# SSM backward by quarters of D, interleaved by priority with the FFN weight-gradient pass; output gradient kept in SBUF; positions split 64x32

## The chip, the cores and the metric

The kernel runs on one core of a Trainium2 chip. The metric is the device time of one execution in microseconds (us). Three executions of the kernel before took 2714.63, 2717.66 and 2719.81 us; the median is 2717.66 us.

## What is computed

The reference is one layer and its gradients, for one sequence of L = 2048 positions, D = 576 channels, N = 128 states per channel and F = 4608 hidden units, all in bfloat16:

```python
xn = layernorm(x)                                   # no weights
K[d,l] = Re( sum_n C[d,n] * exp(dt*A[d,n]*l) * dt*B[d,n] )
s = causal_conv(xn, K) + xn * Dskip                 # by FFT of length 2L in the reference
g = silu( (silu(xn @ w1) * (xn @ w3)) @ w2 )
out = x + s * g
# then the vector-Jacobian product of out with grad_out, with respect to
# x, A_re, A_im, B_re, B_im, C_re, C_im, log_dt, Dskip, w1, w3, w2
```

The outputs are `out` (out_0), the gradient of x (out_1), the gradients of the eight SSM parameters (out_2 to out_9) and those of the three weight matrices (out_10 to out_12).

## The kernel before

The kernel is written in a framework that takes tiles from pools with a fixed number of buffers, finds the dependencies between instructions, orders the instructions of each engine by a priority and sets the semaphores. The order on each engine's queue is fixed before the kernel runs, and every queue is worked off in order. A call of `at(us)` (L81) sets the priority of the instructions that follow it, as a planned time; where no such call is made, program order counts. A tile that is allocated waits for the release of what lay at its address.

Positions are split for the SSM kernel K as l = 128*a + b, with AV = 16 values of a and BV = 128 values of b (L36, L54). For each chunk of 16 channels (36 chunks) a tile of QW + PW = 16*128 + 16*16 = 2304 columns of exponentials (`E_k`, L384 to L387, written to memory early) and of sines and cosines (`kgen_chunk`, L428: the matmul L439, the mask `m_k` on VectorE L440, three passes of ScalarE in `trig`, L294 to L298) is multiplied to `q_k` (the b part, stored to `Q_dram`) and `p_k` (the a part, stored through `pz_k`, which GpSimd makes at L453 and L454, to `PZ_dram`). The matmuls `kps` (L467) give K.

The program runs in these stages, whose times below are read from the trace.

- 0 to 110 us: parameters, layer norm. 110 to 243: `ssm_early` (L359), the exponentials and the spectra `UH_dram` of the input.
- 243 to 920: `ssm_forward` (K by chunks, then the convolution in blocks of 512 by DFT matmuls, L525 and L541, with the complex products of `cmul_acc`, L553, on VectorE) and `ffn_hidden` (L639) are interleaved by `at`.
- 948 to 1105: `ffn_output` (L687), 16 tiles of 128 positions. It forms the output gradient `go_o` and its transpose `gT` (L746, L749), writes them to `GO_dram` and `GOT_dram` (L736, L750), and writes `gs_t` for the SSM side to `GS_dram` (L739).
- 1115 to 1395: `phase5_conv_bwd` (L767), in two halves of 288 channels: DFT of `gs` (L525), products `Z` (L558 to L566) on VectorE, inverse DFT (L541) into `gKK` (the gradient of K) and, with the spectra of K, into the gradient of xn (`gx`, L849 to L851, stored to `GXN_dram`).
- 1395 to 1629: `param_sums` (L862): for each of the 36 chunks `qT` is loaded from `Q_dram` by a transposing DMA (L977), 32 matmuls `pT` of 32 columns sum over b (L879), and VectorE multiplies by `pz` and sums over a (L884, L886) into `S_all`. Then `phase5_final` (L889) makes the parameter gradients.
- 1629 to 2318: `phase6_weights` (L979), the FFN weight-gradient pass, in 18 groups of 256 hidden units: `go_oT` and `go_o` are loaded; per group `phase6_elementwise` (L1005) loads `gg_n` and `h_n`, applies SiLU and its derivative, computes `ph` from `go_oT` and `w2T` (L1038) with five matmuls for each of 16 tiles of positions (four of 128 rows, a tail of 64), and stores `gu_n`, `gg_n` to `GU_dram`, `GG_dram` (L1044); `phase6_weight_grads` (L1047) of the group before follows with the accumulations L1061, L1072, L1079 and L1081. `e_in` has three buffers, so the loads of a group need not wait for the group before; `e_ps_gw` has four PSUM banks.
- 2318 to the end: `phase6_inputs` (L1088): `w1T` and `w3T` are loaded by 72 transposing DMAs of 128 columns of a weight matrix each (L977 from the loop over `fi`), then 16 tiles of 144 matmuls (L1116) and the layer-norm backward.

All transposing DMAs are issued by the SP queue, in order with SP's other loads and stores.

## Time and profile before

| | |
|---|---|
| median of three executions | 2717.66 us |
| the profiled execution: its own time | 2719.59 us |
| its span, first to last instruction | 2717.6 us |
| mean granted TensorE clock | 0.828 |
| TensorE (PE) busy | 2024.5 us, 74% |
| VectorE (DVE) busy | 1418.1 us, 52% |
| ScalarE (ACT) busy | 929.7 us, 34% |
| GpSimd (POOL) busy | 519.0 us, 19% |

All numbers of the trace come from one execution. A row of the windows view gives a stretch of the span, its length, the busy time of each engine in it with the number of its instructions, the granted TensorE clock, the mean busy share of the DMA engines and their rate. A row of the groups gives a line, an engine, an operation and its tiles, the count, the busy time of the group and the mean time of one in ns, and the idle time ahead of it with what ended it. A row of the timeline gives a start, a duration and an instruction.

### The profile page before, as it was taken

Reading aid. Unit: us, or ns where it says so; the run is one execution under the profiler, and the core shown is the slowest. Engines: PE = TensorE matmul, PEld = TensorE weight load, DVE = VectorE, ACT = ScalarE, POOL = GpSimd, SP = SyncE. Lnnn points to the kernel's source line nnn. Section 1 sums busy time; section 2 is a strip of 40 time slices with the busy share of each in tenths; the row PEclk is TensorE's granted clock in tenths of the full one; section 3 lists DMA queues with packets and bytes.
Section 4 is the critical chain, followed back from the end, with each engine's and each line's share of the span. In section 5 each row is a group of like instructions: output and inputs, shape, how many; then the busy total and the mean of one; then the engine's idle time right before and its main releaser. Section 6 shows DMA issues by size and latency. Waiting matters only on the chain.

```text
span 2717.6 us, 37783 instructions
## 1 busy us (share of the span) xinstructions
PE 2024.5 (74%) x14886; PEld 1289.5 (47%) x14886; DVE 1418.1 (52%) x2396; ACT 929.7 (34%) x1203; POOL 519.0 (19%) x763
## 2 busy tenths in 40 slices
PE   1797777878799699636343325999999999129998
PEld 0332322322255277424233312777777778127777
DVE  7312666766687445597978892433333332002222
ACT  1356677777755211212100003444444441000000
POOL 1001454554533411000000000222222222000000
PEclk9555888887899899868665556999999999569999
DMA  3245656666665798323179947655555552488873
GB/s 74 81 191 220 230 203 238 236 220 236 222 232 185 216 236 212 88 63 95 55 176 237 233 106 208 177 158 152 166 166 168 151 153 64 102 164 176 169 165 73
DMA packets 678742, 455.04 MB, mean 167 GB/s; under 512 B 491426, under 2 KB 631972, under 8 KB 669220
## 3 DMA queue, kind: packets, MB, share of 16 engines
q1 hardware_dynamic: 541780, 246.58, 36.6%
q0 software_dynamic: 31824, 109.16, 11.8%
q10 hardware_dynamic: 104960, 96.90, 11.2%
q8 instruction: 116, 1.90, 0.3%
q14 instruction: 62, 0.51, 0.1%
HBM read 132.12 MB, written 209.24 MB: 126 GB/s over the span
## 4 chain that ended last, share of the span: by engine, by line
PE 37%; DVE 9%; DMA 8%; SPq 4%; issue 1%; ACT 0%; POOL 0%; ACTq 0%; DVEq 0%; POOLq 0%
PE px L1116 10%; PE pgw L1072 9%; PE ph L1038 8%; DMA qT<-Q_dram 6%; PE pgw L1061 5%; SPq L977 4%; DVE cm_t L564 1%; PE et_ps L525 1%; PE pgw L1079 1%; DVE Z L562 1%; PE inv_ps L541 1%; DVE cm_t L561 1%; DVE Z L565 1%; DVE Z L566 1%; PE pT L879 1%
## 5 line engine op out<-in xcount | busy, mean ns | idle before, releaser
L1116 PE MATMUL px<-w1T,ggc 128*128 128x288 bf16 x1152 | 236.5, 287 | 103.3 <-DMA ggc<-GG_dram 103.3
L1038 PE MATMUL ph<-w2T,go_oT 128*128 128x256 bf16 (+1 forms) x1440 | 228.9, 282 | 54.8 <-issue 40.4
L1116 PE MATMUL px<-w3T,guc 128*128 128x288 bf16 x1152 | 236.3, 287 | 4.6 <-DMA guc<-GU_dram 4.6
L1072 PEld LDWEIGHTS <-xn_bf 128*128 128x128 bf16 x2304 | 225.4, 98 | 27.0 <-issue 0.8
L671 PE MATMUL pg<-wmB_w,xnT 128*128 128x512 bf16 x576 | 178.7, 432 | 68.8 <-ACT g_t L678 44.5
L671 PEld LDWEIGHTS <-xnT 128*128 128x128 bf16 x1152 | 112.0, 105 | 234.0 <-issue 161.4
L1038 PEld LDWEIGHTS <-go_oT 128*128 128x128 bf16 (+1 forms) x1440 | 117.6, 98 | 164.3 <-issue 117.9
L1120 DVE TENSOR_TENSOR gx<-px,gx 128x288 f32<-128x288 f32 x32 | 13.2, 453 | 329.7 <-PE px L1116 329.7
L671 PE MATMUL pu<-wmB_w,xnT 128*128 128x512 bf16 x576 | 180.7, 430 | 2.0 <-ACT u_t L679 2.0
L1116 PEld LDWEIGHTS <-ggc 128*128 128x128 bf16 x1152 | 113.1, 98 | 132.4 <-issue 103.5
L1040 ACT CAST gh<-ph 128x512 bf16<-128x512 f32 x144 | 80.5, 586 | 257.1 <-PE ph L1038 252.4
L1075 DVE CAST gw<-pgw 128x256 bf16<-128x256 f32 x144 | 60.8, 423 | 202.1 <-PE pgw L1072 156.0
L721 PE MATMUL po<-w2g,hc 128*128 128x288 bf16 x1152 | 146.0, 289 | 27.1 <-DMA hc<-H_dram 27.1
L879 PE MATMUL pT<-gKK,qT 128*128 128x32 bf16 x1152 | 71.7, 233 | 116.6 <-DMA qT<-Q_dram 113.6
L1133 ACT ACTIVATE t<-gx 128x576 f32<-128x576 f32 x16 | 10.9, 683 | 396.8 <-DVE gx L1120 396.8
L1061 PE MATMUL pgw<-go_o,h_n 128*128 128x288 bf16 x1152 | 145.0, 287 | 0.0
L1017 POOL MEMSET w2r<- 128x64 bf16 x36 | 5.7, 158 | 722.8 <-PE pT L879 501.8
L453 POOL COPY pz_k<-p_k 128x512 bf16<-128x512 bf16 x36 | 73.0, 2029 | 353.8 <-DVE p_k L446 353.8
L721 PEld LDWEIGHTS <-hc 128*128 128x128 bf16 x1152 | 112.4, 99 | 57.2 <-issue 27.4
L685 POOL DMA_DIRECT2D G_dram<-g_t x144 | 106.1, 737 | 165.9 <-ACT g_t L678 160.9
L440 DVE TENSOR_SCALAR m_k<-et_ps 128x512 int32<-128x512 int32 (+1 forms) x180 | 103.9, 627 | 53.8 <-PE et_ps L439 53.8
L1041 DVE TENSOR_TENSOR gu_n<-gh,gu_n 128x1024 bf16<-128x1024 bf16 x72 | 49.7, 690 | 154.9 <-ACT gh L1040 154.9
(306 smaller groups left out, 4293.4 us busy)
## 6 DMA issues: line engine op xcount, KB each, us to landing
Q_dram<-q_k ACTq DMA_DIRECT2D x36, 1024.0 KB, 4.6
E_dram<-E_k SPq DMA_DIRECT2D x36, 576.0 KB, 2.7
E_l<-E_dram SPq DMA_DIRECT2D x36, 576.0 KB, 6.0
G_dram<-g_t POOLq DMA_DIRECT2D x144, 128.0 KB, 4.1
U_dram<-u_t POOLq DMA_DIRECT2D x144, 128.0 KB, 4.9
H_dram<-h_t SPq DMA_DIRECT2D x72, 256.0 KB, 5.4
gg_n<-G_dram POOLq DMA_DIRECT2D x18, 1024.0 KB, 5.2
h_n<-U_dram POOLq DMA_DIRECT2D x18, 1024.0 KB, 6.0
```

The lines of the kernel that those rows point to most:

```text
L440: nc.vector.tensor_scalar(out=m[:, o:o + ow], in0=pt[:, 0:ow].bitcast(I32), scalar1=(1 << 16) - 1, scalar2=None, op0=ALU.bitwise_and)
L453: nc.gpsimd.tensor_copy(out=pz[:, 1:3], in_=p[:].rearrange("p r a d -> p r d a"))
L671: nc.tensor.matmul(pt[:], lhsT=xnT[:, c, ts], rhs=wm[w][:, c, :], start=(c == 0), stop=False)
L685: nc.gpsimd.dma_start(out=dst[fb * (FB // self.FG) + k, :, i0:i0 + NT, :], in_=src[:, :, gs])
L721: nc.tensor.matmul(po_[:, pi_, 0:pw], lhsT=hc[:, fi, :], rhs=w2[fi][:, po:po + pw], start=(fi == 0), stop=(fi == FT - 1))
L879: nc.tensor.matmul(pT[:, dl, k, :], lhsT=qT[:, (1 - k) * DC + dl, :], rhs=gKK[:, :, :, d0 + dl], start=True, stop=True)
L977: self.nc.sync.dma_start_transpose(out=dst, in_=src)
L1038: nc.tensor.matmul(ph[:, j, :].rearrange("p (a f) -> p a f", f=P), lhsT=go_oT[0:dsz, c, tt * P:(tt + 1) * P], rhs=w2T[0:dsz, :, c, :], sta ...
L1040: nc.scalar.copy(out=gh[:, t2 * 2:t2 * 2 + 2, :], in_=ph[:])
L1061: nc.tensor.matmul(pgw[pi_][:, 0:pw], lhsT=hn[:, tt, fl * P:(fl + 1) * P], rhs=go_o[:, tt, po:po + pw], start=(tt == 0), stop=(tt == LT - 1))
L1072: nc.tensor.matmul(pw_[:, 0:FG], lhsT=self.xn_bf[:, tt, c * P:(c + 1) * P], rhs=nat[:, tt, :], start=(tt == 0), stop=(tt == LT - 1))
L1116: nc.tensor.matmul(px[pi_][:, 0:pw], lhsT=act[:, fi, :], rhs=wT[:, fi, po:po + pw], start=(fi == 0 and ai == 0), stop=(fi == FT - 1 and ai ...
```

## The change

- **Positions 64x32.** l = 64*a + b: AV = 32, BV = 64. The chunk's tile is 16*64 + 16*32 = 1536 columns. `Q_dram` and `qT` halve, `PZ_dram` and `pz` double. `pz_k` is made by four copies and one negation. `kps` takes 64 matmuls of 64 output rows in place of 32 of 128. The pools `kg_e` and `kg_m` get three buffers in place of two.
- **Channels in a permuted order.** The SSM's scratch arrays hold the channels as four quarters, in each of which 72 channels of the lower and 72 of the upper half of D stand; views `perm` and `nat4` translate. The DMAs of `split_rates` become 54 in place of 45, the skip matmuls of the forward convolution (L544) 192 in place of 96.
- **Output gradient in SBUF.** `go_o`, `goT` and `goTt` are kept in tiles that live through `ffn_output` and the weight-gradient pass; `GO_dram` and `GOT_dram` are gone. `goTt` holds the 64-channel tail of the transpose, tiles 0 to 7 on partitions 0 to 63 and tiles 8 to 15 on 64 to 127. `o_h` goes from four to three buffers, `o_in` from three to two.
- **SSM backward by quarters**, each with its parameter sums, under `at` times that interleave it with the 18 FFN groups. The parameter sums contract 64 positions (two half-height matmuls on row halves) and leave 32 to VectorE.
- **FFN pass.** `e_in` has two buffers in place of three, `e_ps_gw` two banks in place of four. The 64-row tails of `ph` for tiles t and t + 8 stand next to each other on different rows. `GU_dram` and `GG_dram` are stored by twice as many DMAs.
- **`phase6_inputs`.** `w1T` and `w3T` are loaded by ten transposing DMAs of up to 128 rows by 4608 columns. `gxs` is loaded by ScalarE's queue.

The core of the diff:

```diff
-    AV: int = 16
-    BV: int = 128
+    AV: int = 32
+    BV: int = 64
...
-                for c, (do, dsz) in enumerate(cfg.dch):
-                    self.dma(self.PCS_dram[q, k, do:do + dsz, :], pc[0:dsz, k, c, :])
+                for (c, p0, n, h, d1) in self.dsplit():
+                    self.dma(self.PCS_dram[q, k].rearrange("(d h) n -> h d n", h=2)[h, d1:d1 + n, :], pc[p0:p0 + n, k, c, :])
...
-        nc.gpsimd.tensor_copy(out=pz[:, 1:3], in_=p[:].rearrange("p r a d -> p r d a"))
-        nc.gpsimd.tensor_scalar(out=pz[:, 0], in0=pz[:, 2], scalar1=-1.0, scalar2=None, op0=ALU.mult)
+        pv = p[:].rearrange("p r a (g d h) -> p g h r d a", g=2, h=2)
+        for g in range(2):
+            for h in range(2):
+                nc.gpsimd.tensor_copy(out=pz[:, g, h, 1:3], in_=pv[:, g, h])
+        nc.gpsimd.tensor_scalar(out=pz[:, :, :, 0].rearrange("p g h d a -> p (g h) (d a)"),
...
-            for k in range(2):
-                nc.tensor.matmul(kps[:, dl, :], lhsT=q[:, k, dl, :], rhs=v[:, k, :, dl], start=(k == 0), stop=(k == 1))
+            for hf in range(2):
+                for k in range(2):
+                    nc.tensor.matmul(kps[64 * hf:64 * hf + 64, dl, :], lhsT=q[:, k, dl, :],
+                                     rhs=v[:, k, hf * AH:(hf + 1) * AH, dl], start=(k == 0), stop=(k == 1))
...
-                got = ip.tile([P, D], BF16, name="go_o")
+                got = go_o[:, i, :]
-                nc.sync.dma_start(out=self.GO_dram[:, i, :], in_=got[:])
...
+                nc.scalar.copy(out=goT[:, :, i * P:(i + 1) * P], in_=ptr[:, 0:nfull, :])
...
+            for g in range(4):
+                with self.tc.tile_pool(name="b_gk", bufs=1) as gkp:
+                    gK = gkp.tile([P, 2, 2, LT, Wq // 2], BF16, name="gK")
+                    with self.tc.tile_pool(name="b_k", bufs=1) as kp, \
+                            self.tc.tile_pool(name="b_z", bufs=2) as zp:
+                        self.conv_bwd_quarter(g, gK, kp, zp, ps, T0 + g * TQ, TQ * 0.45)
+                    with self.tc.tile_pool(name="g_q", bufs=3) as qp:
+                        self.param_quarter(g, gK, S_all, qp, ps, T0 + (g + 0.45) * TQ, TQ * 0.55)
+            self.at(T0 + 4 * TQ)
+            self.phase5_final(fix, S_all, ps)
...
+            for h in range(2):
+                for hf in range(2):
+                    nc.sync.dma_start(out=gK[64 * h:64 * h + 64, hf, :, i * KT:(i + 1) * KT, :].rearrange(
+                        "p k t d -> p k (t d)"), in_=st[64 * hf:64 * hf + 64, h].rearrange("p k t d -> p k (t d)"))
...
+    def param_quarter(self, g, gK, S_all, qp, ps, T0, TQ):
+        NQ = D // 16 // 4
+        for cc in range(NQ):
+            ch = g * NQ + cc
+            self.at(T0 + TQ * cc / NQ)
+            qT = qp.tile([P, 2, 8, N], BF16, name="qT")
+            self.nat_transpose(qT[:].rearrange("p k d n -> p (k d) n"), self.Q_dram[ch])
+            pz = qp.tile([P, 2, 2, 3, 4, AV], BF16, name="pz")
+            nc.scalar.dma_start(out=pz[:], in_=self.PZ_dram[:, ch])
+            for dg in range(2):
+                T = [ps.tile([P, 2, 4, 2, AV], FP32, name="et_ps") for _ in range(2)]
+                for dd in range(4):
+                    for k in range(2):
+                        for h in range(2):
+                            hs = slice(64 * h, 64 * h + 64)
+                            nc.tensor.matmul(T[h][:, 1 - k, dd].rearrange("p k (f t) -> p k f t", f=2), lhsT=qT[hs, k, d8, :],
+                                             rhs=gK[hs, :, :, :, cc * 8 + d8].rearrange("p f k t -> p k f t"),
+                                             start=True, stop=True)
+                for h in range(2):
+                    for s in range(2):
+                        pr = qp.tile([P, 8, 2, AV], FP32, name="pr_q")
+                        nc.vector.tensor_tensor(out=pr[:], in0=T[h][:].rearrange("p r d k a -> p (r d) k a"),
...
+                        nc.vector.tensor_reduce(out=S_all[:, 2 * s:2 * s + 2, d0:d0 + 4].rearrange("p k d -> p d k"),
+                                                in_=pr[:].rearrange("p (r d) k a -> p d k r a", r=2), op=ALU.add,
...
+    def backward(self, T0, TG, TS, TQ):
+        with self.tc.tile_pool(name="e_w", bufs=2) as wp, \
+                self.tc.tile_pool(name="e_in", bufs=2) as inp, \
+                self.tc.tile_pool(name="e_el", bufs=2) as elp, \
+                self.tc.tile_pool(name="e_gw", bufs=2) as gwp, \
+                self.tc.tile_pool(name="e_ps_h", bufs=3, space=bass.MemoryType.PSUM) as ps_h, \
+                self.tc.tile_pool(name="e_ps_gw", bufs=2, space=bass.MemoryType.PSUM) as ps_gw:
+            self.phase5_ssm_bwd(T0 + TS, TQ)
+            NG = F // self.FG
+            for gi in range(NG + 1):
+                self.at(T0 + TG * gi)
+                if gi < NG:
+                    tiles = self.phase6_elementwise(gi, wp, inp, elp, ps_h)
+                if gi > 0:
+                    self.phase6_weight_grads(gi - 1, prev, self.go_o, gwp, ps_gw)
...
+                    steps = [(self.goT[:, c, tt * P:(tt + 1) * P], w2T[:, :, c, :]) for c in range(nfull)]
+                    steps.insert(nfull * (1 - j), (self.goTt[rs, t * P:(t + 1) * P], w2T[rs, :, nfull, :]))
...
-            for fi in range(FT):
+            for (do, dsz) in cfg.dch:
                 for (w, wT) in (("B_w1", w1T), ("B_w3", w3T)):
-                    self.nat_transpose(wT[:, fi:fi + 1, :], aps[w][:, fi * P:(fi + 1) * P])
+                    self.nat_transpose(wT[:, :, do:do + dsz], aps[w][do:do + dsz, :])
...
-        k.ffn_output(480, 10)
-        k.at(700)
-        k.phase5_ssm_bwd()
         k.parp_ctx.close()
+        with tc.tile_pool(name="go_keep", bufs=1) as gop:
+            k.go_o = gop.tile([P, k.cfg.LT, k.cfg.D], BF16, name="go_o")
+            k.goT = gop.tile([P, k.cfg.D // P, k.cfg.L], BF16, name="goT")
+            k.goTt = gop.tile([P, k.cfg.L // 2], BF16, name="goTt")
+            k.ffn_output(480, 10)
+            k.backward(700, 40, 0, 165)
         mats.close()
-        k.phase6_ffn_bwd()
+        k.phase6_inputs()
```

More of the change, by code (lines that the diff above doesn't have):

```diff
@@ L53, in make @@
         c.M = 2 * LS - 1
-        c.AV = L // P
-        c.BV = P
+        assert L % 64 == 0
+        c.AV = L // 64
+        c.BV = 64
+        assert c.AV % 2 == 0 and c.AV <= 64
         return c
@@ L519, in dft_block @@
         nc, KT = self.nc, self.cfg.KT
[L520 removed]
+        Q, Wq = dst.shape[1], dst.shape[4]
         for kt in range(KT):
@@ new lines, in phase5_ssm_bwd @@
+            for g in range(4):
+                with self.tc.tile_pool(name="b_gk", bufs=1) as gkp:
[5 more added lines that the diff above has]
+                        self.param_quarter(g, gK, S_all, qp, ps, T0 + (g + 0.45) * TQ, TQ * 0.55)
@@ L809, in conv_bwd_half @@
-        gds_sb = sp.tile([1, W], BF16, name="gds_sb")
-        nc.scalar.copy(out=gds_sb[:], in_=gds[:, 0:W])
-        nc.sync.dma_start(out=self.aps["out_9"].rearrange("(o d) -> o d", o=1)[:, cs], in_=gds_sb[:])
+            self.at(T0 + TQ * 0.05 * b)
+            G.append(kp.tile([P, 1, 2, KT, W], BF16, name=f"g_{b}"))
+            self.dft_block(ps, lambda tt: gs[:, b * KT + tt, :], G[b])
+        gds = ps.tile([P, 512], FP32, name="et_ps")
+        for b in range(NB):
+            prod = zp.tile([P, KT, W], BF16, name="gsxn")
+            for tt in range(KT):
+                t = b * KT + tt
+                nc.vector.tensor_tensor(out=prod[:, tt, :].rearrange("p (h d) -> p h d", h=2),
+                                        in0=gs[:, t, :].rearrange("p (h d) -> p h d", h=2),
+                                        in1=self.nat4(self.xn_bf[:, t, :])[:, g], op=ALU.mult)
+            for tt in range(KT):
+                nc.tensor.matmul(gds[0:1, 0:W], lhsT=self.ones_col[:], rhs=prod[:, tt, :], start=(b == 0 and tt == 0),
+                                 stop=(b == NB - 1 and tt == KT - 1))
@@ L812, in conv_bwd_half @@
+        gds_sb = zp.tile([1, W], BF16, name="gds_sb")
+        nc.scalar.copy(out=gds_sb[:], in_=gds[0:1, 0:W])
+        with nc.allow_non_contiguous_dma(reason="small vector store"):
+            nc.sync.dma_start(out=self.aps["out_9"].rearrange("(o h g d) -> o g h d", o=1, h=2, g=4)[:, g],
+                              in_=gds_sb[:].rearrange("p (h d) -> p h d", h=2))
         nxt = None
         for i in range(NB - 1, -1, -1):
-            Z = zp.tile([P, 2, KT, W], BF16, name="Z")
+            self.at(T0 + TQ * (0.2 + 0.1 * (NB - 1 - i)))
+            Z = zp.tile([P, 1, 2, KT, W], BF16, name="Z")
```

469 lines of the change are left out of this document (228 added, 241 removed).

## Prediction

> **What bounds the kernel now.** I read first the table by stages, with the limits of the stages taken from the chain of waits and the timeline. Its columns are the stretch and its length, then the busy time of PE, PEld, DVE, ACT and POOL with the instructions of each, then the granted clock, the DMA share and GB/s.
>
> ```profile
> 110.00:243.00 133.00, 121.41 (x368) 45.77 (x366) 18.19 (x24) 76.77 (x72) 0.00 (x0) 0.50 0.47 190
> 243.00:750.00 507.00, 396.67 (x2343) 149.63 (x2342) 343.19 (x566) 367.22 (x398) 249.94 (x271) 0.81 0.65 228
> 750.00:920.00 170.00, 167.96 (x1036) 89.18 (x1034) 144.91 (x178) 94.21 (x204) 69.47 (x99) 1.00 0.55 195
> ...
> 948.00:1115.00 167.00, 154.36 (x1232) 117.81 (x1232) 89.26 (x136) 23.55 (x49) 20.97 (x39) 0.97 0.87 207
> 1115.00:1395.00 280.00, 135.79 (x799) 88.88 (x800) 239.03 (x288) 51.93 (x130) 0.00 (x0) 0.74 0.27 74
> 1395.00:1590.00 195.00, 75.41 (x1167) 67.97 (x1164) 167.56 (x217) 1.17 (x2) 1.30 (x4) 0.50 1.12 232
> 1590.00:1674.00 84.00, 12.76 (x48) 5.40 (x49) 41.28 (x240) 12.34 (x9) 6.13 (x14) 0.50 0.59 153
> 1674.00:2316.00 642.00, 641.20 (x5398) 478.37 (x5398) 243.33 (x448) 269.87 (x283) 151.91 (x303) 0.99 0.52 149
> 2316.00:2427.00 111.00, 3.13 (x40) 2.12 (x38) 0.85 (x2) 0.00 (x0) 1.62 (x4) 0.52 0.58 121
> 2427.00:2718.00 291.00, 283.83 (x2302) 225.79 (x2300) 62.39 (x128) 12.42 (x32) 0.00 (x0) 0.99 0.70 151
> ```
>
> From 1115 to 1674 us, the SSM backward, DVE leads: 85% busy in the convolution, 86% in the parameter sums, while PE idles and is granted 0.74 and 0.50 of its clock. From 1674 to 2316, the FFN weight gradients, PE is full and DVE 38% busy. These two parts, 1201 us together, are what the change lays over each other. From 2316 to 2427 nothing computes. From 243 to 750 no engine is full (PE 78%, ACT 72%, DVE 68%): there the in-order queues wait for each other. In the chain of waits one FFN group looks like this; the pitch of 1792.64 - 1756.77 = 35.87 us times 18 is the 642 us, all of it PE.
>
> ```profile
> 1756.77 11.86 PE ph L1038 x78
> 1768.63 7.95 PE pgw L1061 x64
> 1776.80 13.97 PE pgw L1072 x128
> 1792.64 11.86 PE ph L1038 x78
> ```
>
> **The combined pass, DVE.** A stage that holds both parts lasts at least as long as its fullest engine. DVE's work of before is 239.03 + 167.56 + 41.28 + 243.33 = 691 us. The change adds to it. The groups below give line, operation, tiles, shape and count, then busy time, the mean ns of one, and idle time.
>
> ```profile
> L884 DVE TENSOR_TENSOR pr_q<-pT,pz 128x512 f32<-128x512 f32 x144 | 93.4, 683 | 24.9 <-PE pT L879 13.9 <-DMA pz<-PZ_dram 10.9
> L886 DVE TENSOR_REDUCE S_all<-pr_q 128x32 f32<-128x1024 f32 x72 | 87.3, 1212 | 0.0
> L564 DVE TENSOR_TENSOR cm_t<-g,az 128x2304 bf16<-128x2304 bf16 x40 | 54.2, 1356 | 0.0
> L565 DVE TENSOR_TENSOR Z<-Z,cm_t 128x1152 bf16<-128x1152 bf16 x40 | 30.2, 755 | 0.3
> L850 DVE TENSOR_TENSOR gx<-inv_ps,gx 128x288 f32<-128x288 f32 x32 | 14.3, 455 | 1.3 <-PE inv_ps L541 1.0
> ```
>
> With 64x32, PE sums 64 positions and DVE has to sum 32 instead of 16. Per chunk there are 2 groups of channels, 2 halves and 2 signs, so 8 products and 8 reductions of 512 elements, where 4 products of 512 and 2 reductions of 1024 stood. That is twice the elements: 288 products at 683 ns and 288 reductions at about half of 1212. The stage's DVE time of 167.56 doubles; I add 175 for the split (bounds 160 to 190). Quarters halve the width of the convolution's instructions and double their count. L565 shows 755 ns for 1152 elements against 1356 for 2304 in L564, so halving costs 755 - 678 = 77 ns an instruction where none overlaps, on some 370 instructions 28 us; in the records neighbours overlap by about 70 ns, so I take 15 (bounds 5 to 30, with the small products and the 64 additions of L850's kind inside). DVE then needs 691 + 175 + 15 = 881 us.
>
> How full can DVE be kept? The stages of before in which it leads or shares the lead with PE give 239.03/280 = 85%, 167.56/195 = 86% and 144.91/170 = 85%. I take 85.5%: 881/0.855 = 1030 us. The bounds are the 98.8% that PE reaches in the interleaved stretch from 750 (167.96/170), which gives 892, and the 67.7% of DVE from 243 to 750, which gives 1301. I take the middle one because the combined pass resembles the stretch from 750 to 920, convolution beside FFN, with two independent threads to fill from. Against 1201 that is **-171 us** (bounds -309 to +100).
>
> **The combined pass, PE and the queues.** PE's work at full clock is 641.2 x 0.99 = 635 us for the FFN, 135.79 x 0.74 = 100 for the convolution and 75.41 x 0.50 = 38 for the sums (the same count of half-height matmuls, 64 columns in place of 32, so up to 75). In the chain above 128 matmuls of 256 columns take 13.97 us, 109 ns each, while 78 of `ph` take 11.86, 152 each; with one tail in five, a tail costs about 0.2 us beyond its columns. Paired tails stand on different rows, and such pairs run side by side already:
>
> ```profile
> 434.80 0.39 PE L672 MATMUL pg<-wtail,xnT 64*128 64x512 bf16 x1
> 434.81 0.39 PE L673 MATMUL pu<-wtail,xnT 64*128 64x512 bf16 x1
> ```
>
> Eight pairs then cost 8 x 0.31 in place of 16 x 0.31, 2.5 us a group, 45 us in all (bound 0, if other work falls between the two). PE needs 635 - 45 + 100 + 38 to 75, 728 to 765, up to 810 without the pairs. At 1030 us that is under 81%, so neither the 45 us nor the following are on the path while DVE leads: with two banks in `e_ps_gw` PE waits twice a group for two ACT copies of 0.4 us, some 30 us; the matmuls of 144 columns in the DFTs are twice as many. The 72 groups of half-height matmuls in the sums may each cost a tail's 0.2 us, 14 us.
>
> The ACT work of both parts and the reload that goes:
>
> ```profile
> L1025 ACT ACTIVATE gu_n<-gg_n 128x4096 bf16<-128x4096 bf16 x18 | 65.1, 3617 | 0.2
> L1065 ACT CAST gw<-pgw 128x288 bf16<-128x288 f32 x72 | 25.3, 402 | 101.2 <-PE pgw L1061 64.6 <-issue 34.4 <-DVE gg_n L1042 2.2
> L1025 ACT ACT_TABLE_LOAD x18 | 23.1, 1283 | 48.2 <-DMA gg_n<-G_dram 47.9
> 1631.15 18.00 DMA go_oT<-GOT_dram
> 1649.40 13.91 DMA gg_n<-G_dram
> ```
>
> ACT has 269.87 + 51.93 + 13.5 = 335 us and 144 more store issues; at a third of the pass it hides them. The new waits: with two buffers in `e_in`, the loads of group g+1 on POOL's queue wait until PE has finished the weight gradients of group g-1, and the loads of `w2r` and the stores of `gw` queue behind them. The load (13.91 us for the first), SiLU and its derivative (2 x 3.6 + 2 x 1.3) and 16 products of 0.7 are 35 us, in the time of one 57 us group (1030/18), so it hides. On SP the loads of a quarter, 64 moves into `gK` and the `qT` transposes stand in one row with `w2T`; each can hold the other thread back. I leave that inside the 85.5%. The reload of `go_oT` at 1631.15 and what waits for it lie inside the 1201.
>
> **Before and after the pass.** The exponentials shrink to two thirds. PE leads that stretch, 121.41 of 133 us, at half its clock.
>
> ```profile
> L384 PE MATMUL e_ps<-SELR,lhs_r 48*128 48x512 bf16 (+1 forms) x180 | 75.6, 581 | 11.6 <-ACT E_k L386 11.6
> L294 ACT ACTIVATE S_k<-m_k,npi_col 128x2304 bf16<-128x2304 int32 x36 | 80.8, 2244 | 2.7 <-DVE m_k L440 2.7
> L467 PE MATMUL kps<-v_k,q_k 128*128 128x16 bf16 x1152 | 49.2, 196 | 21.0 <-DVE v_k L462 21.0
> L453 POOL COPY pz_k<-p_k 128x512 bf16<-128x512 bf16 x36 | 73.0, 2029 | 353.8 <-DVE p_k L446 353.8
> ```
>
> A third of 75.6 is **-25 us** (bound 0, if ACT takes over). In the K chunks, 243 to 750, three trig passes of 2.24 us become 1.5 each: 36 x 3 x 0.75 = 80 us less on ACT, which is the gain if ACT sets the pace. Against it, `kps` doubles its matmuls (+49 us if the column halves do not overlap), the a-part products on DVE double while the b-part and `m_k` shrink (about even), and POOL's copies double. What POOL does there DVE feels: the first `t_k` after the copy starts takes 1330 ns at the median, the second, of the same shape, 611.
>
> ```profile
> L459 DVE TENSOR_TENSOR t_k<-p_k,WrT x36: 609/1330/1344, 261.8 to 740.1; 128x512 bf16<-128x512 bf16 x36
> L459 DVE TENSOR_TENSOR t_k<-p_k,nWiT x36: 412/611/612, 263.8 to 741.3; 128x512 bf16<-128x512 bf16 x36
> 426.80 1.60 DVE L680 TENSOR_TENSOR h_t<-s_t,u_t 128x1024 bf16<-128x1024 bf16 x1
> ```
>
> That is 0.72 us a chunk now; twice to 3.5 times as much on the chain would be +26 to +68 us. The Trainium skill (SBUF — State Buffer, Who interferes with whom) speaks against this part: a DVE instruction with two SBUF inputs and a GpSimd instruction that reads SBUF exclude each other for a whole instruction, so each of the five POOL instructions could hold DVE. The row of `t_k` agrees. With gains of 80 and losses of 49 + 68 on a chain that shows no full engine I take 0 (bounds -80 to +117). The permuted order adds 9 small stores and 96 small matmuls (about 6 us of PE), and the dropped stores of `go_o` save SP time beside a PE that is busy for 154.36 of 167; both 0.
>
> The 72 transposes of `w1T` and `w3T` are set by SP's issue:
>
> ```profile
> L977 SPq DMA_TRANSPOSE w1T<-in_B_w_dram x36: 1162/1264/1267, 2318.7 to 2410.2; - x36
> L977 SPq DMA_TRANSPOSE w3T<-in_B_w_dram x36: 1256/1264/1267, 2320.0 to 2411.5; - x36
> L977 SPq DMA_TRANSPOSE ggc<-GG_dram x16: 4492/4602/5729, 2413.2 to 2657.7; - x16
> 2421.59 0.64 PE L1116 MATMUL px<-w1T,ggc 128*128 128x288 bf16 x2 [103.25 <-DMA ggc<-GG_dram]
> ```
>
> From 2318.7 to the last one's end at 2412.8 they take 94 us. The new ones have the form of `ggc`, 128 rows by 4608: eight at 4.6 to 5.7 and two of half the rows at half to all of that, 41 to 57 us. I take 49: **-45 us** (bounds -53 to -37). The products after it keep their 284 us of PE.
>
> **The sum.** The profiled execution took 2719.59 us (span 2717.6, 2 us around it), against a median of 2717.66. 2719.6 - 171 - 25 + 0 - 45 = **2478.6**, so 2480 us.
>
> **Rivals.** (A) DVE is filled as PE is from 750 to 920: 892 us, total 2719.6 - 309 - 70 = 2341. For it: two threads; against it: both SSM stages left 15% idle at quarter and chunk borders. (B) Slower: the fixed order of the queues decides, as from 243 to 750. DVE stands behind an FFN product whose ACT operand waits for a SiLU block, with only two groups in flight, while finished parameter sums wait behind it. At 67.7% the pass is 1301 us, total 2719.6 + 100 - 70 = 2750. It decides once DVE is under 881/1271 = 69%. Against it: no such loss where FFN and convolution ran together. (C) The K chunks lengthen by POOL's copies, +68: 2548. (D) PE becomes the bound through its clock. It was granted 0.50 at 75.41 busy of 195, 0.74 at 135.79 of 280, 0.81 at 396.67 of 507 and 1.00 at 167.96 of 170; 765 us of work at 0.70 is 1093, total 2542; it decides below 765/1030 = 0.74. The Trainium skill (TensorE: Matmul & The Clock Gate, Part 1) says that an idle window of some 3.4 us brings the clock back to half, which the row at 0.50 bears out and which DVE-bound sums in between would invite. (E) The change does not interleave: one thread's instructions stand ahead of the other's, and the parts follow each other: (239 + 15)/0.85 + (168 + 175)/0.86 + 41 + 597 = 1336, total 2719.6 + 135 - 70 = 2785. Against it: `at` spreads both over the same planned times.
>
> **How the numbers follow.** Forecast 0.46, A 0.15, B 0.11, C 0.14, D 0.10, E 0.04. The forecast's own range is 2420 to 2540. To leave no more than two in ten out I reach past A below, and over C and D and half way to B above: 2330 to 2640. Less than 0.2% is no change that a measurement of this kernel can tell. Faster holds the forecast, A, C and D: 0.85; B and E make slower, of which 0.02 may end within 0.2%: same 0.02, slower 0.13.
>
> **What would show it.** A stage from about 1090 to 2120 with DVE 85% busy, PE 75 to 80% and FFN groups every 57 us between parameter sums; 288 products near 683 ns and 288 reductions near 610; e_ps done 25 us earlier; ten transposes and a gap of 65 us before the last 284. DVE under 69% in that stage, a granted clock under 0.74, or a K stage longer than 507 by tens of us would prove it wrong.

## The result, and the profile after

The changed kernel takes 2550.9 us (median of four runs, 2544.9 to 2558.5) where the kernel before took 2717.4: a ratio of 0.939, with a 95% interval of 0.936 to 0.942. The profiled execution took 2549.0 us with a span of 2547.2.

The table by stages of the changed kernel, with the columns of the one before (stretch, length, busy time of PE, PEld, DVE, ACT and POOL, granted clock, DMA share, GB/s):

```profile
100.00:220.00 120.00, 111.99 (x337) 37.94 (x337) 22.66 (x31) 55.30 (x39) 0.00 (x0) 0.50 0.45 169
220.00:630.00 410.00, 348.89 (x3393) 149.42 (x3392) 345.83 (x490) 296.74 (x389) 324.59 (x374) 0.86 0.69 226
630.00:805.00 175.00, 170.32 (x1143) 92.48 (x1143) 144.04 (x176) 93.51 (x204) 68.66 (x97) 1.00 0.66 197
850.00:1010.00 160.00, 141.89 (x1128) 107.68 (x1126) 88.62 (x130) 26.39 (x51) 25.39 (x48) 0.96 0.79 177
1010.00:2107.00 1097.00, 893.86 (x7809) 675.51 (x7810) 845.05 (x1678) 333.24 (x540) 157.19 (x294) 0.89 0.56 142
2107.00:2150.00 43.00, 11.50 (x86) 8.40 (x84) 32.87 (x164) 1.86 (x4) 2.19 (x4) 0.66 0.11 25
2150.00:2196.00 46.00, 39.51 (x348) 32.27 (x349) 8.86 (x19) 3.55 (x8) 9.71 (x18) 0.88 0.30 92
2196.00:2256.00 60.00, 1.66 (x14) 0.71 (x10) 0.43 (x1) 0.00 (x0) 1.06 (x2) 0.52 1.05 222
2256.00:2547.00 291.00, 284.03 (x2301) 225.84 (x2299) 62.38 (x128) 12.42 (x32) 0.00 (x0) 0.99 0.77 151
1010.00:2196.00 1186.00, 944.87 (x8240) 716.19 (x8242) 886.79 (x1859) 338.65 (x552) 169.08 (x316) 0.88 0.53 136
```

Set beside the stages of before, the rows say where the 170 us of span came from:

| | before | after | difference | predicted |
|---|---|---|---|---|
| start of the combined pass | 1115 | 1010 | -105 | -25 |
| of this, K chunks | 507 | 410 | -97 | 0 |
| the pass (both threads) | 1201 | 1186 | -15 | -171 |
| weights transposed, nothing computed | 111 | 60 | -51 | -45 |
| last products | 291 | 291 | 0 | 0 |

Of the 105 us, the K chunks begin 23 us earlier (220 against 243) and last 97 us less, and the time from their end to the pass grows by 15 (365 to 380). The bounds of the stages are rounded: marked by the first load of `gs`, at 1114.7 and at 1014.6 us, the pass begins 100 us earlier and is 22 us shorter.

The change won, but not where it was expected to. The forward part, which the forecast credited with 25 us, gave 105. The pass, for which most of the change was written, gave 15. Its DVE work is 886.79 us, as forecast (881), but DVE is busy 75% of the time and not 85.5%. Two rows at its end show a tail: for 43 us the short instructions of the final sums run while PE has next to nothing, and then the last FFN group has 46 us to itself.

The groups by line of the changed kernel (busy time, mean ns of one, idle time just before and what ended it), and the waits of DVE and of PE between 1010 and 2196 us (total, times, longest):

```profile
L944 DVE TENSOR_TENSOR pr_q<-et_ps,pz 128x512 f32<-128x512 f32 x288 | 185.5, 683 | 53.9 <-PE et_ps L937 52.8
L947 DVE TENSOR_REDUCE S_all<-pr_q 128x8 f32<-128x512 f32 x288 | 184.2, 678 | 0.0
L499 PE MATMUL kps<-v_k,q_k 128*64 128x16 bf16 x2304 | 58.1, 194 | 58.3 <-DVE v_k L493 49.6 <-DVE v_k L494 8.6
L408 PE MATMUL e_ps<-SELR,lhs_r 48*128 48x512 bf16 x108 | 52.4, 623 | 0.0
```

```profile
DVE gw L1138 <- DMA out_dram<-gw: 75.2, 35, 5.8
DVE pr_q L944 <- PE et_ps L937: 52.8, 37, 11.9
DVE gw L1138 <- PE pgw L1135: 44.0, 30, 10.4
```

```profile
PE pgw L1135 <- DVE gw L1138: 95.3, 22, 22.9
PE ph L1098 <- ACT gh L1101: 35.9, 18, 12.7
```

The longest waits of both engines meet at one instruction: L1138, DVE's copy of a finished w1 or w3 gradient out of a PSUM bank into a buffer `gw`. PE stands 95 us because the copy that frees its bank has not been made. DVE stands 75 us in front of the copy because the store has not emptied the buffer, and 44 us because PE is still filling the bank. The timeline of DVE at one such place:

```profile
1686.92 0.42 DVE L1138 CAST gw<-pgw 128x256 bf16<-128x256 f32 x1
1687.27 0.68 DVE L947 TENSOR_REDUCE S_all<-pr_q 128x8 f32<-128x512 f32 x1
1687.86 0.68 DVE L944 TENSOR_TENSOR pr_q<-et_ps,pz 128x512 f32<-128x512 f32 x1
1690.56 0.42 DVE L1138 CAST gw<-pgw 128x256 bf16<-128x256 f32 x1 [2.02 <-DMA out_dram<-gw]
1690.90 0.68 DVE L947 TENSOR_REDUCE S_all<-pr_q 128x8 f32<-128x512 f32 x1
```

The reduction at 1690.90 has had its operand since the product of 1687.86 ended. It waits 2 us for a store of the other thread, only because a gradient copy stands ahead of it in DVE's queue.

### The profile page after: what moved, and what is told of

It is laid out like the page before. It is cut to its first block, busy times and chain, and to the rows that moved or that the text cites. A ratio compares the mean times of both kernels' runs of the same rounds, so it can differ in the third digit from the quotient of the medians.

```text
span 2547.2 us, 42384 instructions
## 1 busy us (share of the span) xinstructions
PE 2045.9 (80%) x16790; PEld 1356.5 (53%) x16790; DVE 1615.1 (63%) x2986; ACT 846.5 (33%) x1299; POOL 607.8 (24%) x871
## 4 chain that ended last, share of the span: by engine, by line
PE 28%; DVE 16%; issue 13%; DMA 9%; SPq 4%; ACT 3%; POOL 1%; ACTq 1%; POOLq 0%; DVEq 0%
PE px L1180 11%; PE ph L1098 4%; SPq L1056 3%; PE et_ps L937 3%; PE pgw L1124 3%; DMA out_dram<-gw 2%; DMA w2T<-w2r 2%; DVE cm_t L602 2%; PE et_ps L578 2%; PE pgw L1135 2%; DVE pr_q L944 1%; DVE gg_n L1084 1%; DVE cm_t L599 1%; PE pg L718 1%; DVE h_n L1085 1%
## 5 line engine op out<-in xcount | busy, mean ns | idle before, releaser
L1135 PE MATMUL pgw<-gu_n,xn_bf 128*128 128x256 bf16 x1152 | 166.8, 306 | 78.1 <-DVE gw L1138 75.0
L944 DVE TENSOR_TENSOR pr_q<-et_ps,pz 128x512 f32<-128x512 f32 x288 | 185.5, 683 | 53.9 <-PE et_ps L937 52.8
L1098 PE MATMUL ph<-w2T,goT 128*128 128x256 bf16 x1152 | 190.1, 296 | 11.6 <-DMA w2T<-w2r 7.6
L1184 DVE TENSOR_TENSOR gx<-px,gxs 128x288 f32<-128x288 f32 x32 | 13.2, 453 | 280.7 <-PE px L1180 280.7
L947 DVE TENSOR_REDUCE S_all<-pr_q 128x8 f32<-128x512 f32 x288 | 184.2, 678 | 0.0
L1139 POOL DMA_DIRECT2D out_dram<-gw x144 | 77.5, 540 | 429.0 <-DVE gw L1138 408.4
L937 PE MATMUL et_ps<-gK,qT 64*128 64x64 bf16 x1152 | 133.8, 289 | 39.7 <-DMA GU_dram<-gu_n 15.1
L1124 PE MATMUL pgw<-go_o,h_n 128*128 128x288 bf16 x1152 | 159.6, 288 | 1.6 <-DVE gw L1147 0.7
L1098 PEld LDWEIGHTS <-goT 128*128 128x128 bf16 x1152 | 101.9, 103 | 94.3 <-issue 55.9
L1135 PE MATMUL pgw<-gg_n,xn_bf 128*128 128x256 bf16 x1152 | 133.2, 276 | 20.2 <-DVE gw L1138 20.2
L1138 DVE CAST gw<-pgw 128x256 bf16<-128x256 f32 x144 | 59.3, 421 | 121.7 <-DMA out_dram<-gw 75.2
```

The source lines that it names most:

```text
L937: nc.tensor.matmul(T[h][:, 1 - k, dd].rearrange("p k (f t) -> p k f t", f=2), lhsT=qT[hs, k, d8, :], rhs=gK[hs, :, :, :, cc * 8 + d8].rear ...
L944: nc.vector.tensor_tensor(out=pr[:], in0=T[h][:].rearrange("p r d k a -> p (r d) k a"), in1=pz[:, dg, h, s:s + 2].rearrange("p r d a -> p ...
L947: nc.vector.tensor_reduce(out=S_all[:, 2 * s:2 * s + 2, d0:d0 + 4].rearrange("p k d -> p d k"), in_=pr[:].rearrange("p (r d) k a -> p d k ...
L1098: nc.tensor.matmul(ph[j][:, k, :].rearrange("p (a f) -> p a f", f=P), lhsT=lw, rhs=rh, start=(n == 0), stop=(n == nfull))
L1124: nc.tensor.matmul(pgw[pi_][:, 0:pw], lhsT=hn[:, tt, fl * P:(fl + 1) * P], rhs=go_o[:, tt, po:po + pw], start=(tt == 0), stop=(tt == LT - 1))
L1135: nc.tensor.matmul(pw_[:, 0:FG], lhsT=self.xn_bf[:, tt, c * P:(c + 1) * P], rhs=nat[:, tt, :], start=(tt == 0), stop=(tt == LT - 1))
```

## The experiments

In each experiment, the edit changes the planned order of instructions somewhat, since the order is planned anew for every kernel. Times are medians, and ratios are to the kernel before.

**e1. More buffers for the finished gradients.**

```diff
-tc.tile_pool(name="e_gw", bufs=2)
+tc.tile_pool(name="e_gw", bufs=4)
```

> The changed kernel with four buffers instead of two in the pool of the finished weight gradients (e_gw). In the combined pass DVE waits 75 us for a gw buffer that a store has not left yet, and PE waits 95 us for the bank that DVE then frees late. Theory 'small buffers hold the pass': both waits go, the pass shortens by 40 to 85 us, time 2465 to 2510 us, DVE fill from 75% to 79% or more. Rival 'the order of the two threads holds it': DVE waits a little later for the next thing instead, time 2535 to 2555.

Measured 2524.8 us, ratio 0.930 (0.928 to 0.931): 26 us less, less than the theory's 40. DVE's waits in the pass of this kernel:

```profile
DVE pr_q L944 <- PE et_ps L937: 72.4, 48, 14.1
DVE gw L1138 <- PE pgw L1135: 64.7, 51, 10.3
DVE gw L1138 <- DMA out_dram<-gw: 5.2, 4, 1.6
```

The wait for the store is gone (75.2 to 5.2 us). More than half of it came back as a longer wait for PE, at the copy (44.0 to 64.7) and at the products (52.8 to 72.4). DVE's fill rose only from 75% to 76%. Both theories had a part of it.

**e2. Half of the parameter sums left out.** **e8. Half of the w1 and w3 products left out.** Together they weigh DVE and PE.

```diff
-                    for s in range(2):                       # e2
+                    for s in range(1):
-                for tt in range(LT):                         # e8
+                for tt in range(0, LT, 2):
```

> The changed kernel without the second half of the parameter sums (one of the two products with their reductions, 144 of each left out; that half of S_all is set to zero, so the parameter gradients are not computed in full). It takes 144 x (0.683 + 0.678) = 196 us of DVE work away and nothing from the other engines. Theory of the prediction 'DVE sets the pass': 196 us of work at a fill of 75% are 262 us, the time falls to about 2290 (2355 if only the work itself goes). Rival 'the FFN thread sets it' (18 groups of 62 us, each a chain through DMA, ACT, DVE and PE): time 2500 or more. In between: both share.

> The changed kernel without every other position tile in the gradients of w1 and w3 (half of the products of 128 x 256, so these two gradients are sums over half the positions). It takes about 125 us of PE work at full clock away (1152 x 0.109) and nothing from DVE. Together with e2 it weighs the two engines: if DVE alone set the pass, nothing happens (2545 to 2560); if PE and the FFN chain set it, the time falls by 100 to 150 us (2400 to 2450); if the pass hops from one to the other, by a part of it, as e2 did with 68 of 196 us (2480 to 2520).

Measured: e2 2482.7 us, 68 less for 196 us of DVE work (the sum of the instructions' times; DVE's busy time falls by 171, since neighbours overlap); e8 2511.9 us, 39 less for about 125 us of PE work. The whole pass of e2, and then of e8:

```profile
1010.00:2127.00 1117.00, 961.67 (x8234) 714.26 (x8236) 716.28 (x1571) 338.92 (x552) 165.82 (x316) 0.86 0.56 144
```

```profile
1010.00:2160.00 1150.00, 851.79 (x7092) 621.49 (x7092) 885.36 (x1859) 343.18 (x553) 166.53 (x316) 0.83 0.53 141
```

A microsecond of DVE work is worth 0.35 us of time (0.40 by the busy time) and a microsecond of PE work 0.31. Both times lie where a share of both engines was expected. Neither engine sets the pass by itself. With DVE's work cut by a fifth its fill falls from 75% to 64%, so the forecast's model of "DVE's work divided by a fill" doesn't describe it. Whether the pass hops from one engine to the other or both wait in the same chain, these two runs don't tell; e6 and e12 do that.

**e3, e4, e5. What shortened the K chunks.** Before the change, ACT issued the store of `q_k`, which has to wait until DVE has made `q_k`. The change moved it to SP, in one line that neither the list of changes nor the prediction names. ACT's queue before, in its timeline and its waits from 243 to 750 us:

```profile
426.71 0.67 ACT L674 ACTIVATE s_t<-pg 128x512 bf16<-128x512 f32 x1
426.92 0.36 ACTq L451 DMA_DIRECT2D Q_dram<-q_k  x1
431.78 0.37 ACT L468 CAST KT<-kps 128x256 bf16<-128x256 f32 x1 [4.41 <-PE kps L467]
```

```profile
ACT KT L468 <- PE kps L467: 116.8, 34, 5.7
```

Nothing runs on ACT from 427.4 to 431.8: the store is followed in the queue by the copy of `kps`, and the sine pass of the next chunk stands behind both. The idle time is booked on the copy, which waits for PE. The three edits:

```diff
 # e3, on the changed kernel
-tc.tile_pool(name="kg_e", bufs=3), tc.tile_pool(name="kg_m", bufs=3)
+tc.tile_pool(name="kg_e", bufs=2), tc.tile_pool(name="kg_m", bufs=2)
-        nc.sync.dma_start(out=self.Q_dram[ch], ...)
+        nc.scalar.dma_start(out=self.Q_dram[ch], ...)
 # e4, on the kernel before
-        nc.scalar.dma_start(out=self.Q_dram[ch], ...)
+        nc.sync.dma_start(out=self.Q_dram[ch], ...)
 # e5, on e3: the sine pass of a chunk twice
+        nc.scalar.activation(out=S[:], in_=m[:], func=ACT.Sin, ...)
         nc.scalar.activation(out=S[:], in_=m[:], func=ACT.Sin, ...)
```

> The changed kernel with two details of the K chunks as they stood before: two buffers instead of three for E and m, and the store of q issued by ACT instead of SP. No engine's work changes by more than the 36 issues. Theory 'the chain between the queues set that stage' (before, ACT stood 127 us in front of the copy of kps with the next chunk's trigonometry behind it): the stage of 410 us goes back by 60 to 97 us, time 2610 to 2650. Rival 'the smaller trigonometry passes gave the 97 us': under 15 us, time 2550 to 2565.

> The kernel before with one edit: the store of q in the K chunks is issued by SP instead of ACT. (A third buffer doesn't fit there.) Theory 'the chain between the queues': ACT no longer stands before the store until DVE has made q, the K stage of 507 us shortens by 20 to 60 us, time 2657 to 2697. Rival 'the smaller passes': no change within 0.3%, 2710 to 2725.

> The kernel of e3 (two buffers, store of q issued by ACT) with one more trigonometry pass a chunk: the sine pass is issued twice, 36 x 1.59 = 57 us more on ACT, so that a chunk's passes are about as long as before the change. With it the four cases of short or long passes and of the store on ACT or SP are complete (before: long, ACT; e4: long, SP; e3: short, ACT). Theory 'the store on ACT costs only where the passes are long': the stage of 410 us goes to 460 or more, time 2590 to 2640. Rival 'ACT has slack, the length of the passes doesn't matter in the new chunks': time 2535 to 2560.

The copies of `kps`, one a chunk, mark the stage from its first chunk to its last. Their rows before the change and in e4:

```profile
L468 ACT CAST KT<-kps x36: 372/372/373, 266.6 to 744.3; 128x256 bf16<-128x256 f32 x36
```

```profile
L468 ACT CAST KT<-kps x36: 372/372/373, 265.9 to 662.9; 128x256 bf16<-128x256 f32 x36
```

and in the changed kernel, in e3 and in e5:

```profile
L502 ACT CAST KT<-kps x36: 372/372/402, 234.7 to 629.7; 128x256 bf16<-128x256 f32 x36
```

```profile
L502 ACT CAST KT<-kps x36: 372/372/373, 237.7 to 610.4; 128x256 bf16<-128x256 f32 x36
```

```profile
L504 ACT CAST KT<-kps x36: 362/372/373, 237.5 to 665.4; 128x256 bf16<-128x256 f32 x36
```

| kernel | trigonometry of a chunk | store of q on | first to last copy, us | time, us |
|---|---|---|---|---|
| before | 3 x 2.24 | ACT | 478 | 2717.4 |
| e4 | 3 x 2.24 | SP | 397 | 2635.6 |
| e5 | 4 x 1.59 | ACT | 428 | 2595.3 |
| e3 | 3 x 1.59 | ACT | 373 | 2535.8 |
| after | 3 x 1.59 | SP | 395 | 2550.9 |

The row of e3 comes from an execution of 2545.2 us, 9 above its median.

One line in the kernel before is worth 80 us (ratio 0.971, 0.969 to 0.972), more than the 20 to 60 expected: with it the old chunks, long passes and all, go as fast as the new ones. ACT's wait for `kps` falls, and a sine pass now runs ahead of the copy:

```profile
ACT KT L468 <- PE kps L467: 50.1, 35, 3.4
```

```profile
420.08 2.25 ACT L294 ACTIVATE S_k<-m_k,npi_col 128x2304 bf16<-128x2304 int32 x1
424.05 0.37 ACT L468 CAST KT<-kps 128x256 bf16<-128x256 f32 x1 [1.72 <-PE kps L467]
```

Whether the store's own wait for `q_k` held ACT, or the order that was planned around the store, no run separates.

In the new chunks the store on ACT, together with two buffers, costs nothing: e3 is 15 us faster than the changed kernel, against its theory. It makes two edits at once, so neither has a price of its own; what else differs in e3 stands in the last section. e5 shows when ACT matters. With the store on ACT, 57 us more of passes lengthen the stage by 55, so there the added ACT time comes out one for one. Long passes and the store in one queue were thus a main cause of the long old stage, and the change took away both. They are not the whole of it. e5 stays 50 us under the old stage (428 against 478), and its passes are only 13 us shorter (6.36 against 6.72 us a chunk). The rest is open; the new chunks also have shorter masks and make `q_k` ahead of `p_k`. What was expected of e5 came out at the lower edge (2595 where 2590 to 2640 was said).

**e6. The gradient copies on ACT.** On e1, with four buffers:

```diff
-                nc.vector.tensor_copy(out=gw[:], in_=pw_[:, 0:FG])
+                nc.scalar.copy(out=gw[:], in_=pw_[:, 0:FG])
...
-        nc.vector.tensor_copy(out=gw[:], in_=pw_[:, 0:FG])
+        nc.scalar.copy(out=gw[:], in_=pw_[:, 0:FG])
```

> The kernel of e1 (four buffers for the gradients) with the 162 copies of finished w1 and w3 gradients out of PSUM made by ACT instead of DVE. It moves about 65 us of work from DVE to ACT, which is 28% busy in the pass, and takes DVE's place in the chain that frees a bank for PE. Theory 'each thread waits in the other's queue': PE no longer waits 74 us for a copy that stands behind parameter sums on DVE, and DVE no longer stands 65 us in front of a bank that PE is still filling; time 2525 to at most 2480, down to 2430. Rival 'the fill stays at 75% whatever is moved': only the 65 us of work x some part, or ACT blocks in its turn; time 2500 to 2530.

Measured 2430.2 us, ratio 0.896 (0.893 to 0.898): 95 us less than e1. The pass, and the waits of PE in it:

```profile
1010.00:2080.00 1070.00, 926.69 (x8244) 706.94 (x8241) 828.57 (x1698) 393.44 (x713) 170.82 (x317) 0.91 0.57 151
```

```profile
PE ph L1098 <- ACT gh L1101: 35.7, 12, 12.5
PE et_ps L560 <- ACT g L564: 20.3, 13, 4.5
```

The wait of PE for the copy, 95 us in the changed kernel, is no longer among its long ones, and the granted clock was 0.91, against 0.88 in the changed kernel and 0.86 in e1. ACT had the room: 393 us of work in 1070.

**e12. The work given back elsewhere.** In e6 59 us of work left DVE as well as a place in the chain, so e12 gives DVE 59 us of instructions in the other thread, 144 copies that nothing waits for:

```diff
+                    scr = qp.tile([P, 4, 2, AV], BF16, name="scr")
+                    nc.vector.tensor_copy(out=scr[:], in_=T[h][:, 0])
                     for s in range(2):
```

> The kernel of e6 with DVE's freed work given back at another place: beside the parameter sums DVE makes 144 copies of 128 x 256 out of PSUM into a scratch tile that nothing reads (144 x 0.41 = 59 us, the size of the copies that went to ACT). They stand in the SSM thread, and no bank of the FFN thread waits for one. e6 took 95 us off e1 by moving 59 us of work. Theory 'it was the place in the queue, not the work': by e2's price (68 us for 196 us of DVE work, 0.35 each) this costs 20 us, time 2440 to 2460. Rival 'it was the work': the gain goes again, time 2500 to 2525.

Measured 2455.2 us, ratio 0.904 (0.903 to 0.906): 25 us of the 95 came back, near the 20 that e2's price said. The pass:

```profile
1010.00:2100.00 1090.00, 928.74 (x8234) 705.85 (x8236) 874.29 (x1842) 397.80 (x713) 180.61 (x316) 0.90 0.56 148
```

With nearly the DVE work of the changed kernel (874 against 887 us) the pass is 1090 us long instead of 1186 and DVE 80% full instead of 75%. DVE's busy time rose by 46 us over e6 and not by the whole 59. At the same rate all of it would have cost 32 us, so 60 to 70 of e6's 95 us belong to the place of the copies in the queues, not to their work.

**e7. The final sums last.**

```diff
-            self.at(T0 + 4 * TQ)
+            self.at(T0 + 900)
```

> The changed kernel with the planned time of the final sums put behind the last FFN group (900 in place of 660 after the start of the pass), nothing else. Now 164 short DVE instructions of the final sums (43 us, PE 27% busy) stand ahead of the last group's work, whose 46 us follow alone. Theory 'these 89 us are a tail made by order': the final sums move under the last group and under the 60 us in which the weights are transposed, 30 to 43 us less, time 2508 to 2521. Rival 'they only move': the last group needs DVE too, or the final sums' pools hold up the next stage's memory; 2540 to 2560.

Measured 2530.2 us, ratio 0.931 (0.929 to 0.933): 21 us less, where 30 to 43 were expected. The end of the pass in this kernel:

```profile
2090.00:2130.00 40.00, 36.17 (x304) 27.61 (x303) 25.59 (x92) 16.64 (x19) 6.48 (x12) 0.96 0.44 126
2130.00:2170.00 40.00, 30.65 (x295) 25.68 (x293) 33.68 (x192) 2.75 (x7) 9.43 (x17) 0.97 0.41 52
2170.00:2240.00 70.00, 3.38 (x14) 1.91 (x15) 0.00 (x0) 0.00 (x0) 0.00 (x0) 0.50 1.10 204
```

The final sums now share the last 80 us with the last group, and both engines work. The pass ends 26 us earlier, but the first product of the next stage starts at 2233, only 18 us earlier than the 2251 of the changed kernel.

**e9. The two threads in turn.**

```diff
-            k.backward(700, 40, 0, 165)
+            k.backward(1400, 40, -700, 165)
```

> The changed kernel with the FFN groups planned behind the whole SSM backward (from 700 us after its start) instead of beside it; nothing is added or left out. It prices the interleaving by itself. If the two threads really share the pass now, the parts in turn take (239 + 15)/0.85 + 343/0.86 + 43 for the SSM backward and 597 to 642 for the FFN, 1338 to 1383 us in place of 1186, time 2700 to 2750. If the interleaving gives little because each thread waits in the other's queue: 2600 to 2650. No gain at all from it would be 2550.

Measured 2769.7 us, ratio 1.020 (1.018 to 1.022): above the upper edge of what was expected, and slower than the kernel before. The SSM backward with what FFN work was ready, and then the rest of the FFN:

```profile
1010.00:1790.00 780.00, 441.45 (x3950) 346.55 (x3951) 700.62 (x1513) 135.41 (x337) 45.25 (x75) 0.68 0.43 109
1790.00:2418.00 628.00, 521.55 (x4289) 394.65 (x4290) 186.00 (x347) 202.51 (x214) 123.97 (x241) 0.93 0.44 121
```

So the interleaving does work: it takes 219 us off these same instructions. The Trainium skill (Perfetto Trace Analysis, Optimization Strategy) says that where different stages have different most-contended engines, interleaving the stages may help; the two rows, DVE at 90% and then PE at 83%, and the 219 us agree. About a quarter of the FFN work already runs in the first row (410 of the 1440 `ph` products), so e9 is not a full separation. The pass still gained only 15 us on the kernel before, because e9's two rows together, 1408 us, are 207 more than the 1201 of the old parts. The new form of the SSM backward brings 196 us more DVE work (887 against 691) and half-height products with it; no run prices the two apart.

**e10, e11. Together.** e10 has e6, e7 and e3's chunks in one. e11 is e6 with the final sums last and a slower plan for the SSM thread (180 us a quarter in place of 165).

> The edits that helped, together: gradient copies on ACT with four buffers (e6), final sums planned last (e7), and the K chunks with two buffers and the store of q on ACT (e3, 15 us below the changed kernel, in its K stage). If they add up: 2430 - 20 - 15 = 2395 us. Rival: in e6 the final sums end 48 us before the last group does, so that moving them gives nothing any more; 2415.

> The kernel of e6 with the final sums last and the SSM thread planned at 180 instead of 165 us a quarter, so that both threads are planned to end at 720 us. In e6 the SSM thread ended at 1984 and the FFN thread at 2080, with PE 64% busy in the last 100 us. Theory 'the tail is an idle DVE at the end of the pass': 20 to 40 us less than e6, 2390 to 2410. Rival 'the order inside the pass sets it, not its end': within 15 us of e6, 2415 to 2445.

e10 took 2402.8 us, ratio 0.884 (0.882 to 0.886), 148 us under the changed kernel, between the forecast 2395 and the rival's 2415: the edits beside e6 gave 27 us of the 35 summed. It is the fastest form measured here. e11 took 2435.7 us (median of six, 2416.8 to 2445.5), no gain on e6. In the profiled execution, its fastest, the FFN groups end near 2027, where the transposes of the weights begin, but the final sums then end at 2106, and the last stage's products wait until 2119. The idle end had only changed threads.

## Why the prediction was right or wrong

The sign was right. The measured time lies 71 us above the point 2480 and 11 above the forecast's own range of 2420 to 2540, inside the wide range of 2330 to 2640. That it came so near is luck in part: two large errors had opposite signs. By the measured terms, 2478.6 - 80 (forward) + 156 (pass) - 6 (transposes) = 2548.6.

- **DVE's work in the pass: right.** 881 us forecast, 886.8 measured; products at 683 ns as said, reductions at 678 instead of half of 1212.
- **DVE's fill: the step that failed.** 85.5% was taken from stages in which one thread or two ran without sharing a chain of short buffers; measured 75%. The sentence that failed counts the two banks of `e_ps_gw` among what is not on the path: "neither the 45 us nor the following are on the path while DVE leads". The prediction saw PE wait there for ACT's copies of 0.4 us; it overlooked that the w1 and w3 copies are DVE's and stand behind parameter sums. e1, e6 and e12 show it: the buffers for finished gradients give 26 us, the place of the copies 60 to 70 more, and the fill reaches 80% with nearly the same work. The number of banks was not varied. Of the remaining 5 points up to 85.5%, a part is the end of the pass: in e12 its last 50 us hold 15 us of DVE work, and without them the fill is 83%. The rest isn't explained by a run.
- **"A stage lasts its fullest engine's work over a fill": wrong in form.** e2 and e8 price a microsecond of either engine at 0.3 to 0.4.
- **PE's work: too low.** 728 to 765 us, at most 810 without the pairs; 944.87 x 0.88 = 831 measured. The mis-sized term is the parameter sums, put at 38 to 75 us. Their row in the pass of the changed kernel gives 133.8, about 118 at the granted clock of 0.88:

```profile
L937 PE MATMUL et_ps<-gK,qT 64*128 64x64 bf16 x1152 | 133.8, 289 | 39.7 <-DMA GU_dram<-gu_n 15.1 <-DMA pz<-PZ_dram 11.8 <-DMA qT<-Q_dram 7.4
```

- **K chunks: forecast 0 with bounds -80 to +117, measured -97.** The step weighed engines' work and left out an edit of the diff, the move of the store of `q_k` to SP, which is worth 80 us in the old chunks (e4). The gain came by the wait for `kps` on ACT's queue, not by a sum of engine times. The +49 for `kps` didn't come: 2304 products cost 58.1 us where 1152 cost 49.2, and in the trace every second product starts 3 to 7 ns after the one before, so the column halves overlap.
- **Exponentials and transposes: right.** -25 forecast, 75.6 - 52.4 = 23 measured in `e_ps`. For the weights -45 forecast and -51 measured; the ten transposes run from 2196.5 to about 2245, 49 us as said.
- **Pairs of tails: half right.** In the trace 76 of the 144 pairs start 3 to 4 ns apart, and between the others an FFN or SSM product falls, so about half of the 45 us came.
- **Buffers of `e_in`:** not tried by themselves. DVE's waits for SiLU blocks come to 34 us in the pass; whether the two buffers cause them isn't shown.
- **Rivals.** None came as written. B came nearest to the mechanism, an FFN instruction in front of finished parameter sums, and priced it too high (1301 us, 1186 measured); but the instruction was the gradient copy (DVE's waits there are 119 us), not a product that waits for ACT (35 us). C named the measured total (2548) for a stage that in fact got shorter. D needed a clock under 0.74, and 0.88 was granted. E priced parts in turn at 2785; e9, which comes near that kernel, took 2770.

## What to carry to other kernels

When two threads share in-order queues, list for every PSUM bank which engine frees it and what stands ahead of that instruction in its queue; put the copy on the engine with room, not on the one that both threads need. A fill factor read from other stages need not hold where two threads share buffers and queues (85.5% expected here, 75% measured); leaving out a known amount of one engine's work tells what that engine's microsecond is worth. And cost every moved DMA issue: a store on a computing engine's queue waits there for its data, with the next tile's work behind it (36 stores, 80 us in e4).

## What the runs showed of the hardware that was not expected

**Most half-height products with their own weights do not run two at a time here.** The prediction allowed for the parameter sums' products of 64 rows by 64 columns to cost no more than the old ones. In the timeline of the changed kernel eight of them take 1.09 us, 136 ns each, and 24 in a row take 2.01 us, 84 ns each. A timeline row of the kernel before, at a granted clock of 0.50, has 28 of 128 rows by 32 columns in 1.75 us, 63 ns each:

```profile
1711.90 0.80 PEld L937 LDWEIGHTS <-qT 64*128 64x128 bf16 x8 [0.22 <-issue]
1711.90 1.09 PE L937 MATMUL et_ps<-gK,qT 64*128 64x64 bf16 x8
```

```profile
1695.10 2.01 PE L937 MATMUL et_ps<-gK,qT 64*128 64x64 bf16 x24
```

```profile
1453.48 1.75 PE L879 MATMUL pT<-gKK,qT 128*128 128x32 bf16 x28 [2.69 <-DMA qT<-Q_dram]
```

By the start times in the trace, 137 of the 1152 start about 10 ns after the one before, side by side with it, nearly all of them in rows of 24; most of the others start about 115 ns after it. What keeps these apart (the weights' loading, the strided operand from `gK`, or the order) was not tried.

**DVE products beside POOL's copies lost more time than before, and what that cost is open.** In the K chunks of the changed kernel these DVE products have a fastest, a median and a slowest time that lie far apart:

```profile
L490 DVE TENSOR_TENSOR t_k<-p_k,WrT x36: 676/1131/2706, 229.1 to 623.4; 128x1024 bf16<-128x1024 bf16 x36
L493 DVE TENSOR_TENSOR v_k<-t_k x36: 411/860/911, 231.8 to 626.1; 128x512 bf16<-128x512 bf16 x36
L473 DVE TENSOR_TENSOR q_k<-E_l,S_k x36: 675/1082/1129, 223.4 to 618.4; 128x1024 bf16<-128x1024 bf16 x36
```

About 0.45 us is lost in each of four instructions a chunk (two `t_k`, two `v_k`) and 0.4 in this `q_k`, some 80 us over 36 chunks by the medians. Before, the two `t_k` lost 0.72 and 0.20 us a chunk, 33 us, and `v_k` none. That fits the rule which the prediction cited (the Trainium skill, SBUF — State Buffer, Who interferes with whom), though no run took POOL's copies away. Rival C had priced the growth at 26 to 68 us of time; the stage became 97 us shorter all the same, so such a loss has to be read at the wait that sets the stage. That doesn't make it free. In e3 the same `q_k` loses nothing:

```profile
L473 DVE TENSOR_TENSOR q_k<-E_l,S_k x36: 673/675/684, 224.9 to 599.7; 128x1024 bf16<-128x1024 bf16 x36
```

There the eight products of a chunk (`q_k`, `p_k`, `t_k`, `v_k`) take 212.5 us over all chunks in place of 235.1, and the stage is 22 us shorter (373 against 395). The sizes agree, but e3 also moves a store and takes away two buffers, so the cause isn't shown.
